# Router of a fused attention and expert kernel: each VectorE operation with at most one operand in SBUF, the rest in PSUM; mask, 1e-9 and counts folded into other tiles

## The chip, the cores and the metric

The kernel runs on one core of a Trainium2 chip. The metric is the device time of one execution in microseconds (us). The engines are named as the profile names them: PE (TensorE, with PEld for its weight loads), DVE (VectorE), ACT (ScalarE), POOL (GpSimd) and SP (SyncE, which here only issues DMAs). Each engine works through its own instructions in order. A VectorE operation reads and writes SBUF or PSUM; PSUM has eight banks of 2 KB per partition, and TensorE writes its results there.

## The reference

Attention with pooled queries, followed by a layer of eight experts, of which each token uses one:

```
q_pool = q.reshape(8, 8, 576, 2, 64).mean(axis=3)           # 8 batches, 8 heads, 576 queries, 1152 keys
attn   = softmax(q_pool @ k.T / 8)                          # sum + 1e-9 in the denominator
x      = (attn @ v) as [4608, 512]                          # 4608 tokens
logits = x @ w_gate                                         # [4608, 8]
e_idx  = argmax(logits)
probs  = exp(logits - max);  probs /= probs.sum(-1) + 1e-9
eom    = 1 / (1 + exp(-(x @ w_output_gate)))
out[t] = probs[t, e] * eom[t, e] * (relu(x[t] @ w1[e]) @ w2[e]),   e = e_idx[t]
```

All of it is float32. The kernel splits each matmul operand into a high and a low part.

## The kernel before

The program has an attention stage and an expert stage behind it.

**Attention.** The work is 32 pairs (a batch and two heads, four pairs to a batch). A pair has 18 score steps (two heads times nine chunks of 128 keys). In a score step PE computes scores for 128 keys and 576 queries into a tile `sps` (L277, L279; two such tiles exist), ACT takes the exponential twice (to `ph`, 16 bits, and to full precision, L291 and L292 or L283 and L284), and the difference `pl` is made by POOL (L293) or, in six steps of a pair, by DVE (L287). Four steps later PE multiplies `ph` and `pl` with the values (L306 to L308) in bursts of three chunks. Ahead of the scores, by some 15 steps, a generator `mgen` computes row maxima of the next pair: PE writes a tile `mp` of 128 queries by 384 keys (L230), and DVE reduces it (L231). After five or four query tiles the maxima are transposed by PE (L257), split by DVE into two rows `mr` (L260, L261) and sent by SP into two rows of the operand `qb` (a DMA `qb<-mr`), which the first score step of the next pair needs (L279).

**PSUM.** All the small products share a pool `ps_m` of three banks with the tag `mp`: `mp` itself, the transposed maxima, the transposes and logits of the router, the rank counts. A tile is held from its first write to its last use in program order; a new tile takes a bank that is free by then, and PE waits until that bank's last reader has run.

**Router.** When a batch's attention is done, `logits` (L357) and then `router` (L393) run as generators: at each score step the generator goes on to its next `yield`, and after a `yield 1` it goes on only in a step with a burst. Its instructions stand at the end of the step's. The router transposes the logits of 576 tokens into `tl` (L401), finds the best expert of each token by comparisons and reductions of tiles of 128 partitions by 40 (five groups of tokens by eight experts), all of them in SBUF, and makes a one-hot tile in 16 bits, `ohb` (L436). PE counts with it the rank of each token within its expert (L445 to L448, tile `rk`, with the counts so far, `cum`, cast to `cb`, L438). From this come a slot number `posi`, a gate factor in column 512 of the token rows `xb` (L449), the DMA of these rows to DRAM (`xrows`, L453, L454), the new counts `cum` (L459) and five indirect DMAs that scatter token numbers to their slots (L471), one every three steps. Tokens that a group holds twice are taken out by a `mask` (L432) and by a large number `moob` in their slot (L467). Seven of the eight routers run under the next batch's attention. The eighth runs after the last score step, on its own, and with it the first expert tile waits.

**Order.** PE, DVE, ACT and POOL take their instructions in the order in which the main loop and its generators issue them; `prep_at` places the loads and splits of the pair after next by a table. SP's order follows from the order of the issues.

**Experts.** Tiles of 256 tokens are gathered by slot, multiplied by the weights of their expert (L753, L765 to L767) and scattered to the output. An early tile's gather is set up in the sixth batch's router (`setup`, L617), so that PE has work while the last router finishes.

## Time and profile before

| | |
|---|---|
| time, median of 3 runs | 1728.94 us (1724.48 to 1751.34) |
| the profiled execution | 1714.96 us |
| its span, first to last instruction | 1713.2 us |
| PE busy | 1549.7 us (90%) |
| DVE busy | 1125.6 us (66%), 2246 instructions |
| ACT busy | 1083.1 us (63%) |
| POOL busy | 995.4 us (58%) |

A group of instructions is shown with its line, engine, operation, `out<-in`, count, busy time, mean length of one in ns, and then the idle time of the engine ahead of it with what ended that. In a piece of the timeline a row holds start and length in us, and in brackets the idle time before it. SPq is the queue in which SP issues DMAs. The PE clock is given as a share of full speed.

### The profile page before, as it was taken

To read this page: it belongs to the slowest core of one execution; us is meant where nothing else is said; L and a number is where in the kernel's file an instruction comes from. 1 tells how busy PE (TensorE), PEld (TensorE's weight loads), DVE (VectorE), ACT (ScalarE), POOL (GpSimd) and SP (SyncE) were. 2 spreads that over 40 slices of the span, in tenths; PEclk is the share of its full clock that TensorE was granted. 3 is DMA by queue.
4 is the path that set the end of the run, shared out by engine and by line. 5 is a ranking of instruction groups with operands and counts; after the bars stand their busy time and mean duration, and the time that the engine had idled before them with its cause. 6 is when DMAs were issued, how large, how long until landed. Compare 5 with 4: busy or idle time off the path is not lost. (4 is left out here: it accounts for less than half of the span.)

```text
span 1713.2 us, 42162 instructions
## 1 busy us (share of the span) xinstructions
PE 1549.7 (90%) x16618; PEld 1415.5 (83%) x16618; DVE 1125.6 (66%) x2246; ACT 1083.1 (63%) x1862; POOL 995.4 (58%) x918
## 2 busy tenths in 40 slices
PE   3999988988999898999899889887999999999997
PEld 3888878877888887888888888776899999999996
DVE  3666676675677667667667767766466666666663
ACT  2787777776777777777687767773345444445441
POOL 4678768867777777876777786753322232322210
PEclk8999999999999999999999999988899999999998
DMA  8445554555445644556445653452753663553500
GB/s 215 132 110 148 160 135 106 142 155 138 117 110 163 146 134 133 123 152 167 111 111 144 160 149 106 106 149 78 266 185 129 210 219 123 169 185 127 194 33 23
DMA packets 86401, 242.52 MB, mean 142 GB/s; under 512 B 14314, under 2 KB 15018, under 8 KB 86194
## 3 DMA queue, kind: packets, MB, share of 16 engines
q1 hardware_dynamic: 76474, 218.74, 45.3%
q0 software_dynamic: 9728, 21.05, 3.8%
q8 instruction: 134, 2.20, 0.6%
q14 instruction: 65, 0.53, 0.2%
HBM read 164.70 MB, written 21.17 MB: 108 GB/s over the span
## 5 line engine op out<-in xcount | busy, mean ns | idle before, releaser
L293 POOL TENSOR_TENSOR pl<-p,ph 128x576 f16<-128x576 f32 x381 | 489.9, 1293 | 263.1 <-ACT ph L292 197.7
L231 DVE TENSOR_REDUCE pm<-mp 128x1 f32<-128x384 f32 x864 | 454.2, 550 | 176.5 <-PE mp L230 172.3
L277 PE MATMUL sps<-qa,ka 128*128 128x288 f32 x1152 | 278.7, 324 | 99.4 <-DVE pl L287 47.9
L291 ACT ACTIVATE p<-sps 128x576 f32<-128x576 f32 x381 | 248.4, 652 | 161.3 <-PE sps L279 151.0
L230 PE MATMUL mp<-ka,qa 128*128 128x384 f32 x960 | 317.1, 346 | 10.4 <-DMA qa<-yq 7.9
L277 PEld LDWEIGHTS sps<-qa,ka 128*128 128x128 f32 x1152 | 189.0, 192 | 145.0 <-ACT ph L292 65.5
L306 PE MATMUL av<-vt,ph 128*128 128x65 f16 x2880 | 291.6, 195 | 0.0
L308 PE MATMUL av<-vt,pl 128*128 128x65 f16 x2880 | 289.7, 194 | 0.6 <-POOL pl L293 0.5
L307 PE MATMUL av<-vt,ph 128*128 128x64 f16 x2880 | 290.1, 196 | 0.0
L306 PEld LDWEIGHTS <-ph 128*128 128x128 f16 x2880 | 268.7, 99 | 25.5 <-issue 24.8
L308 PEld LDWEIGHTS <-pl 128*128 128x128 f16 x2880 | 268.4, 100 | 0.9 <-POOL pl L293 0.8
L307 PEld LDWEIGHTS <-ph 128*128 128x128 f16 x2880 | 268.3, 98 | 0.0
L279 PE MATMUL sps<-qb,kb 68*128 68x288 f32 x1152 | 250.9, 300 | 15.8 <-DMA qb<-mr 15.7
L230 PE MATMUL mp<-kb,qb 66*128 66x384 f32 x768 | 264.3, 344 | 0.6 <-DMA kb<-kp 0.6
L292 ACT ACTIVATE ph<-sps 128x576 f16<-128x576 f32 x381 | 246.5, 647 | 0.0
L279 PEld LDWEIGHTS sps<-qb,kb 68*128 68x128 f32 x1152 | 188.8, 193 | 18.0 <-DMA qb<-mr 17.6
L753 PE MATMUL hps<-xh,w1h 128*128 128x256 f32 x704 | 200.1, 284 | 0.0
L283 ACT ACTIVATE ph<-sps 128x576 f16<-128x576 f32 x195 | 127.6, 654 | 114.5 <-PE sps L279 111.5
L753 PE MATMUL hps<-xl,w1h 128*128 128x256 f32 x704 | 199.9, 284 | 0.0
L753 PE MATMUL hps<-xh,w1l 128*128 128x256 f32 x704 | 199.3, 283 | 0.0
L230 PEld LDWEIGHTS mp<-ka,qa 128*128 128x128 f32 x960 | 181.4, 193 | 14.8 <-issue 8.0
L756 ACT ACTIVATE hh<-hps 128x512 fp32r<-128x512 f32 x88 | 52.7, 598 | 220.7 <-PE hps L753 203.0
(174 smaller groups left out, 3219.3 us busy)
## 6 DMA issues: line engine op xcount, KB each, us to landing
ka<-xk SPq DMA_DIRECT2D x128, 288.0 KB
raw1b<-in_w_dram SPq DMA_DIRECT2D x24, 1024.0 KB
raw2b<-in_w_dram SPq DMA_DIRECT2D x24, 1024.0 KB
raw1a<-in_w_dram SPq DMA_DIRECT2D x22, 1024.0 KB
raw2a<-in_w_dram SPq DMA_DIRECT2D x22, 1024.0 KB
qp<-in_qT_dram SPq DMA_DIRECT2D x32, 576.0 KB
kpf<-in_kT_dram SPq DMA_DIRECT2D x32, 576.0 KB
vp<-in_vL_dram SPq DMA_DIRECT2D x32, 576.0 KB
```

The lines of the kernel that those rows point to most:

```text
L230: nc.tensor.matmul(mp, lhsT=l, rhs=r, start=j == 0, stop=j == len(ops) - 1)
L231: nc.vector.tensor_reduce(out=pm[:, i:i + 1], in_=mp, axis=AX.X, op=ALU.max)
L277: nc.tensor.matmul(sps[:, j, 0:288], lhsT=ka[:, h, ks], rhs=qa[:, o + 288 * j:o + 288 * j + 288], start=True, stop=False)
L279: nc.tensor.matmul(sps[:, j, 0:288], lhsT=kb[:, h, ks], rhs=qb[:, h, 288 * j:288 * j + 288], start=False, stop=True)
L283: nc.scalar.activation(out=ph2, in_=x, func=AF.Exp, scale=1.0 / 16)
L291: nc.scalar.activation(out=p32.rearrange("p (j n) -> p j n", j=2), in_=x, func=AF.Exp, scale=1.0 / 16)
L292: nc.scalar.activation(out=ph2, in_=x, func=AF.Exp, scale=1.0 / 16)
L293: nc.gpsimd.tensor_tensor(out=pl, in0=p32, in1=ph, op=ALU.subtract)
L306: nc.tensor.matmul(av_[:, qb, 0:65], lhsT=hi, rhs=vt[:, h, c, 0:65], start=c == 0 and qb == 0, stop=False)
L307: nc.tensor.matmul(av_[:, qb, 0:64], lhsT=hi, rhs=vt[:, h, c, 66:130], start=False, stop=False)
L308: nc.tensor.matmul(av_[:, qb, 0:65], lhsT=lo, rhs=vt[:, h, c, 0:65], start=False, stop=c == NC - 1 and qb == 4)
L753: nc.tensor.matmul(hp[:, f], lhsT=W1[w][:, c, fs], rhs=d[x][:, c], start=i == 0, stop=i == 11)
```

## The change

Only the router and what feeds it change. The logits `lg`, the comparison `eq`, the index `em`, the sums `sx`, `ps`, `cs` and the ranks with offsets `r1` move from SBUF tiles into free columns of the two PSUM tiles `tl` and `rk` (`cut` makes such a view), so that no VectorE operation has two SBUF operands. The one-hot comparison writes 16 bits at once (L432 of the changed kernel); the mask goes, since `moob` is added to `em` before the comparison (L429). The 1e-9 is a ninth column of two lasting tiles `exg`, set once. The counts `cum` are kept in 16 bits, so that PE reads them as they are. There are fewer yields: the rank counts come six steps earlier, the row DMA about five steps earlier, and the five scatters begin nine steps earlier, in the router's own pair.

```diff
-        mask = bp.tile([128, 5, 8], F32, name="mask")
...
-            nc.gpsimd.memset(mask, 1.0)
-            nc.gpsimd.memset(mask[0:64, 4], 0.0)
+            for x in exg:
+                nc.gpsimd.memset(x, 1e-9)
...
+        exg = [bp.tile([128, 5, 9], F32, name=f"exg{i}") for i in range(2)]
...
+            def cut(x, o, *shape):
+                n = math.prod(shape)
+                v = x[:, o:o + n]
+                return v.rearrange("p (t e) -> p t e", e=shape[-1]) if len(shape) == 2 else v
...
-            nc.vector.tensor_copy(out=lg, in_=tv[:, :, 0:16])
-            nc.vector.tensor_tensor(out=lg, in0=lg, in1=tv[:, :, 16:32], op=ALU.add)
+            tv = cut(tl, 0, 5, 32)
+            lg = cut(tl, 160, 5, 16)
+            lh = sm.tile([128, 5, 16], F32, name="lg", bufs=2)
+            V.tensor_copy(out=lh, in_=tv[:, :, 0:16])
+            V.tensor_tensor(out=lg, in0=lh, in1=tv[:, :, 16:32], op=ALU.add)
             yield
             g, og = lg[:, :, 0:8], lg[:, :, 8:16]
+            eq = cut(tl, 248, 5, 8)
...
+            V.tensor_reduce(out=mx, in_=g, axis=AX.X, op=ALU.max)
+            ex = exg[b % 2]
+            V.tensor_tensor(out=ex[:, :, 0:8], in0=g, in1=b8(mx), op=ALU.subtract)
             yield
-            eq = sm.tile([128, 5, 8], F32, name="eq", bufs=2)
-            nc.vector.tensor_tensor(out=eq, in0=g, in1=b8(mx), op=ALU.is_equal)
...
+            V.tensor_tensor(out=eq, in0=g, in1=b8(mx), op=ALU.is_equal)
+            nc.scalar.activation(out=ex[:, :, 0:8], in_=ex[:, :, 0:8], func=AF.Exp)
+            e2 = sm.tile([128, 5, 8], F32, name="eq", bufs=2)
+            V.tensor_tensor(out=e2, in0=eq, in1=em8, op=ALU.mult)
             yield
...
+            em = cut(tl, 288, 5)
+            V.tensor_reduce(out=em, in_=e2, axis=AX.X, op=ALU.min)
+            V.tensor_tensor(out=em, in0=em, in1=moob, op=ALU.add)
             yield
...
-            nc.vector.tensor_tensor(out=oh, in0=em8, in1=b8(em), op=ALU.is_equal)
-            nc.vector.tensor_scalar(out=sx, in0=sx, scalar1=1e-9, scalar2=None, op0=ALU.add)
-            yield
+            ohb = sm.tile([128, 5, 8], BF16, name="ohb", bufs=2)
+            V.tensor_tensor(out=ohb, in0=em8, in1=b8(em), op=ALU.is_equal)
             so = sm.tile([128, 5, 8], F32, name="so", bufs=2)
-            nc.vector.tensor_tensor(out=so, in0=oh, in1=og, op=ALU.mult)
...
-            nc.vector.tensor_tensor(out=oh, in0=oh, in1=mask, op=ALU.mult)
...
-            nc.vector.tensor_copy(out=ohb, in_=oh)
-            cb = sm.tile([128, 8], BF16, name="cb", bufs=2)
-            nc.vector.tensor_copy(out=cb, in_=cum)
...
+            V.tensor_tensor(out=so, in0=og, in1=ohb, op=ALU.mult)
             yield 1
-            rk = ps_m.tile([128, 512], F32, name="tp", tag="mp")
+            rk = psum()
...
+            nc.tensor.matmul(rv, lhsT=ones, rhs=cum.unsqueeze(1).broadcast_to([128, 5, 8]), start=False, stop=True)
+            sl = sm.tile([128, 5], F32, name="sl", bufs=2)
+            V.tensor_reduce(out=sl, in_=so, axis=AX.X, op=ALU.add)
+            nc.scalar.activation(out=sl, in_=sl, func=AF.Exp, scale=-1.0)
+            yield
+            r1 = cut(rk, 40, 5, 8)
+            V.tensor_tensor(out=r1, in0=rv, in1=eoff, op=ALU.add)
+            r2 = sm.tile([128, 5, 8], F32, name="r1", bufs=2)
+            V.tensor_tensor(out=r2, in0=r1, in1=ohb, op=ALU.mult)
+            yield
+            sx = cut(rk, 80, 5)
+            V.tensor_reduce(out=sx, in_=ex, axis=AX.X, op=ALU.add)
+            V.scalar_tensor_tensor(out=sx, in0=sl, scalar=1.0, in1=sx, op0=ALU.add, op1=ALU.mult)
+            V.reciprocal(out=xb[:, :, 512], in_=sx)
...
+            ps = cut(rk, 88, 5)
+            V.tensor_reduce(out=ps, in_=r2, axis=AX.X, op=ALU.add)
...
+            V.tensor_tensor(out=pi, in0=ps, in1=moob, op=ALU.add)
+            yield
...
+            cs = cut(rk, 96, 8)
+            V.tensor_reduce(out=cs, in_=ohb.rearrange("p t e -> p e t"), axis=AX.X, op=ALU.add)
+            V.tensor_tensor(out=cum, in0=cs, in1=cum, op=ALU.add)
...
-        cum = kp.tile([128, 8], F32, name="cum")
+        cum = kp.tile([128, 8], BF16, name="cum")
```

**Where instructions move.** In the lists below L is the line in the kernel's own file, so the two columns of numbers differ by a few. The first place is DVE in the third batch's router, in the score steps in which the one-hot tile is made. `pl` (L287) is the tile that releases a score tile, `pm` (L231) the reduction that releases a bank of `ps_m`. Before:

```order
L231 TENSOR_REDUCE pm<-mp_6730 128x1
L428 TENSOR_TENSOR so<-oh,lg 128x40
L287 TENSOR_TENSOR pl<-sps_6723,ph 128x576
L231 TENSOR_REDUCE pm<-mp_6752 128x1
L231 TENSOR_REDUCE pm<-mp_6757 128x1
L431 TENSOR_REDUCE sl<-so 128x5
L432 TENSOR_TENSOR oh<-oh,mask 128x40
L231 TENSOR_REDUCE pm<-mp_6777 128x1
L436 CAST ohb<-oh 128x40
L438 CAST cb<-cum 128x8
L231 TENSOR_REDUCE pm<-mp_6798 128x1
```

The same engine at the same place of the changed kernel, where a `tp` among the operands of the router is the PSUM tile `tl` or `rk`:

```order
L231 TENSOR_REDUCE pm<-mp_6629 128x1
L432 TENSOR_TENSOR ohb<-em_72,tp 128x40
L434 TENSOR_TENSOR so<-tp,ohb 128x40
L231 TENSOR_REDUCE pm<-mp_6650 128x1
L231 TENSOR_REDUCE pm<-mp_6654 128x1
L444 TENSOR_REDUCE sl<-so 128x5
L375 TENSOR_TENSOR xl<-tp,xh 128x256
L231 TENSOR_REDUCE pm<-mp_6729 128x1
L448 TENSOR_TENSOR tp<-tp,eoff 128x40
L450 TENSOR_TENSOR r_6735<-tp,ohb 128x40
L287 TENSOR_TENSOR pl<-sps_6722,ph 128x576
```

The two casts are gone, the product `so` stands three steps earlier, and between it and the next `pl` stand the rank operations L448 and L450.

The second place is DVE some steps earlier in the same router, behind the end of a value product (L315 to L321 finish it). Before:

```order
L321 TENSOR_TENSOR xb<-av_6310,r 128x5x64
L411 TENSOR_TENSOR eq<-lg,mx 128x40
L413 TENSOR_TENSOR exg<-lg,mx 128x40
L231 TENSOR_REDUCE pm<-mp_6607 128x1
L231 TENSOR_REDUCE pm<-mp_6611 128x1
L260 TENSOR_SCALAR mr<-tp 4x128
```

After:

```order
L321 TENSOR_TENSOR xb<-av_6301,r 128x5x64
L422 TENSOR_TENSOR tp<-tp,mx 128x40
L425 TENSOR_TENSOR eq<-tp,em_72 128x40
L231 TENSOR_REDUCE pm<-mp_6599 128x1
L231 TENSOR_REDUCE pm<-mp_6603 128x1
L260 TENSOR_SCALAR mr<-tp 4x128
```

Two router operations stand ahead of the two reductions in both. But `tl` is in use here now (it is `tp` in L422), and only two banks of `ps_m` are left to the `mp` tiles and the transposed maxima: from `tl`'s transposes to L434, and again from the rank counts to L467, a stretch of some 20 tiles of the pool in each router.

The third place is SP's queue in the pair of the same router. Before:

```order
L99 DMA ka_119<-xk_6599 64x1152
L127 DMA vp<-in_vL_dram 128x1152
L99 DMA ka_119<-xk_6599 64x1152 x3
L99 DMA qa_122<-xq 64x576
L99 DMA qb_125<-xq 64x576
L453 DMA xrows<-xb 128x4x513
L454 DMA xrows<-xb 64x513
```

After:

```order
L99 DMA ka_119<-xk_6591 64x1152
L457 DMA xrows<-xb 128x4x513
L458 DMA xrows<-xb 64x513
L127 DMA vp<-in_vL_dram 128x1152
L99 DMA ka_119<-xk_6591 64x1152 x3
L99 DMA qa_122<-xq 64x576
L99 DMA qb_125<-xq 64x576
```

The row DMA moves ahead of a value load and five operand DMAs. What follows in both is another `qa` and `qb` and then the two DMAs `qb<-mr`.

42 lines of the change are left out of this document (4 added, 38 removed).

## The prediction

> **What bounds the kernel now.** I read busy time by stage first, then the list of waits of PE.
>
> ```profile
> 41.00:1165.00 1124.00, 1012.01 (x13168) 926.08 (x13168) 775.67 (x1809) 832.13 (x1536) 830.17 (x741) 0.98 0.52 134
> 1205.00:1713.00 508.00, 496.01 (x3207) 452.75 (x3205) 308.77 (x332) 228.59 (x288) 127.65 (x118) 0.99 0.45 155
> PE sps L277 <- DVE pl L287: 47.9, 67, 1.6
> PE sps L277 <- ACT ph L292: 46.2, 61, 1.0
> PE sps L279 <- DMA qb<-mr: 15.7, 8, 7.6
> ```
>
> The first two rows are stretches (start and end, length, then busy time of PE, PEld, DVE, ACT and POOL), the others who waited for whom, with total, count and longest. PE sets the time. In the stage of the experts (1205 to 1713) it works 496 of 508 us, and the change touches nothing there. In the attention stage it works 1012 of 1124 us, and most of the 112 us that it lacks are waits for a score tile to come free, from DVE (47.9 us) or ACT (46.2 us). So a router costs time only where its work on DVE delays something that PE waits for. What one costs is read from the length of a pair, from its first exponential to that of the next pair:
>
> ```profile
> 460.56 0.65 ACT L291 ACTIVATE p<-sps 128x576 f32<-128x576 f32 x1
> 494.21 0.65 ACT L291 ACTIVATE p<-sps 128x576 f32<-128x576 f32 x1
> 530.75 0.65 ACT L291 ACTIVATE p<-sps 128x576 f32<-128x576 f32 x1 [0.20 <-PE sps L279]
> ```
>
> The pair from 460.56 has no router and takes 33.65 us (494.21 − 460.56); the next has the third batch's and takes 36.54. A router under attention costs 2.9 us, seven of them 20 us, about 1.2% of the time: that caps what can be won there. The groups and a piece of the timeline show what in the router is slow.
>
> ```profile
> L436 DVE CAST ohb<-oh 128x40 bf16<-128x40 f32 x8 | 10.1, 1266 | 0.0
> L438 DVE CAST cb<-cum 128x8 bf16<-128x8 f32 x8 | 9.0, 1123 | 0.0
> L428 DVE TENSOR_TENSOR so<-oh,lg 128x40 f32<-128x40 f32 x8 | 8.0, 995 | 0.0
> L461 DVE TENSOR_TENSOR r<-r,oh 128x40 f32<-128x40 f32 x8 | 1.5, 184 | 0.0
> L451 DVE TENSOR_TENSOR r<-tp,eoff 128x40 f32<-128x40 f32 x8 | 1.3, 163 | 0.1
> 509.31 1.11 DVE L428 TENSOR_TENSOR so<-oh,lg 128x40 f32<-128x40 f32 x1
> 512.87 1.42 DVE L436 CAST ohb<-oh 128x40 bf16<-128x40 f32 x1
> 514.21 1.26 DVE L438 CAST cb<-cum 128x8 bf16<-128x8 f32 x1
> 509.12 1.24 POOL L192 TENSOR_TENSOR vt<-vp,vt 128x576 f16<-128x576 f32 x1
> 512.82 1.43 POOL L137 TENSOR_TENSOR yq<-qp 128x576 f32<-128x576 f32 x1
> 514.20 1.25 POOL L192 TENSOR_TENSOR vt<-vp,vt 128x576 f16<-128x576 f32 x1
> ```
>
> Forty elements take 184 ns in L461 and about 1000 to 1270 ns in the two casts and `so`. Each of the three slow ones starts just behind the start of a POOL operation and ends with it (509.12 + 1.24 = 510.36 against 509.31 + 1.11 = 510.42; 514.25 against 514.29; 515.45 against 515.47). They don't compute longer, they wait for POOL. L461 has the same two SBUF operands as `so` and met no POOL operation.
>
> **The change part by part.** *The waits for POOL.* The casts are gone, and `so` gets one PSUM operand. How much of the 3.4 us of these three reaches PE is read by setting the router's pair beside the plain one, matmul by matmul:
>
> ```profile
> 511.24 0.50 PE L277 MATMUL sps<-qa,ka 128*128 128x288 f32 x2 [1.21 <-DVE pl L287]
> 515.08 0.51 PE L277 MATMUL sps<-qa,ka 128*128 128x288 f32 x2
> 517.52 0.50 PE L277 MATMUL sps<-qa,ka 128*128 128x288 f32 x2 [0.74 <-DVE xl L376]
> 476.27 0.50 PE L277 MATMUL sps<-qa,ka 128*128 128x288 f32 x2 [0.58 <-DVE pl L287]
> 480.11 0.51 PE L277 MATMUL sps<-qa,ka 128*128 128x288 f32 x2
> 481.25 0.43 PE L277 MATMUL sps<-qa,ka 128*128 128x288 f32 x2
> ```
>
> Behind `so`, the `pl` that frees a score tile comes late: PE waits 1.21 us instead of 0.58, 0.63 lost. Behind the casts PE needs 2.44 us from one score step to the next (515.08 to 517.52) instead of 1.14: 1.30 lost. Together 1.93 us of the router's 2.9; the rest is mostly PE's own work for it and stays. Seven routers: −13.5 us. This supposes that the new forms do not wait. L451, with one operand in each memory, averaged 163 ns over eight routers, so none of its eight met such a wait; what the SBUF-only reductions and the 16-bit one-hot do beside POOL I take to be the same. The page "SBUF — State Buffer" of the Trainium skill, section "Who interferes with whom", says that an operation with at most one SBUF input, outside the two-port copy modes, does not contend with GpSimd; by that all 20 operations of the new router are free, and the slow rows above agree with its other half.
>
> *The price of a PSUM operand.* 163 ns (L451) against 184 (L461): nothing, at −21 ns for each. The rule that speaks against this change stands in "VectorE: DVE Perf Modes" of the Trainium skill, section "The TRN2 errata": 120 cycles fixed for a PSUM source against 58 from SBUF. At its 0.96 GHz that is an estimated 65 ns for each operation, 0.9 us of DVE per router for some 14 operations, and 6 us in all if PE waited for all of it. The rows say the opposite sign, and I take zero.
>
> *The banks.* This is new work for PE's waits. With `tl` in use, the transposed maxima (L257) must take the bank of the first of the two `mp` tiles just ahead of it, not the third one:
>
> ```profile
> 502.63 0.27 PE L257 MATMUL tp<-ident,m 128*4 128x128 f32 x1
> 504.77 0.53 PE L277 MATMUL sps<-qa,ka 128*128 128x288 f32 x2 [0.76 <-ACT ph L292]
> 502.42 0.34 DVE L411 TENSOR_TENSOR eq<-lg,mx 128x40 f32<-128x40 f32 x1
> 502.79 1.01 DVE L231 TENSOR_REDUCE pm<-mp 128x1 f32<-128x384 f32 x2
> 503.52 0.65 ACT L291 ACTIVATE p<-sps 128x576 f32<-128x576 f32 x1
> ```
>
> The reduction of that tile is the first of the two at 502.79 and ends at about 503.3 (half of 1.01). So L257 goes at 503.35 instead of 502.63, 0.72 us late. Queued behind it on PE is the next score step; ACT starts on that at 503.52 with no idle time before it, and PE waits for ACT's result at 504.77. Nothing on that way has slack, so the 0.72 us is paid in full. In the second hold, that of `rk`, I find one more place: a sum, a product and a reciprocal now stand ahead of a reduction, some 0.6 us by the steps of the last router below; the tile that needs the bank comes later, and I count an estimated 0.15 us of it. Together 0.87 us per router, +6.1 us for seven. The bounds: nothing, if the banks fall otherwise; 3.9 us per router, if six more of the some 20 tiles in the two holds lose 0.5 us each (the rival below).
>
> *The row DMA and the scatters.* Each pair's first score step needs `qb<-mr`:
>
> ```profile
> 387.39 0.50 PE L279 MATMUL sps<-qb,kb 68*128 68x288 f32 x2 [1.57 <-DMA qb<-mr]
> 247.18 0.50 PE L279 MATMUL sps<-qb,kb 68*128 68x288 f32 x2 [0.66 <-DMA qb<-mr]
> 521.93 0.39 SPq L453 DMA_DIRECT2D xrows<-xb  x1
> 525.77 1.59 SPq L99 DMA_DIRECT2D qb<-mr  x2
> ```
>
> The list of waits has 15.7 us of this, of which 7.6 is the start of the program; 8.1 us are left in seven waits. Two of them, 1.57 and 0.66, stand at the end of a router's pair, where the row DMA (over 1 MB: 512 rows of 513 floats) is issued 3.8 us ahead of `qb<-mr`. The change issues it ahead of six more DMAs, so it should be through: −2.2 us. Behind it in SP's queue `vp` and `ka` wait for the reciprocal; they have a pair's time. In return the first scatter moves into the same place. Bounds: −8.1, if all seven waits go, and +8, if as many come. I take −2.
>
> *The last router* has nothing beside it:
>
> ```profile
> 1171.36 0.24 DVE L403 COPY lg<-tp 128x80 f32<-128x80 f32 x1 [0.61 <-PE tp L401]
> 1171.64 0.24 DVE L404 TENSOR_TENSOR lg<-lg,tp 128x80 f32<-128x80 f32 x1
> 1172.26 0.20 DVE L413 TENSOR_TENSOR exg<-lg,mx 128x40 f32<-128x40 f32 x1
> 1172.38 0.20 DVE L416 TENSOR_TENSOR eq<-eq,em 128x40 f32<-128x40 f32 x1
> 1175.32 1.28 DVE L741 TENSOR_TENSOR xl<-xps,xh 128x512 fp32r<-128x512 f32 x2
> 1176.73 0.19 PE L784 MATMUL cp<-cb,ones 128*128 128x8 bf16 x1 [2.48 <-DVE cb L782]
> ```
>
> Operations that depend on the one before start some 0.25 us after it (1171.36, 1171.64), others 0.12 (1172.26, 1172.38). Before, L741, on which PE's restart waits, starts 3.96 us after L403. After, the chain has 15 dependent and four free steps ahead of the last one, 15 × 0.25 + 4 × 0.12 = 4.2, and L741 follows 0.12 later: +0.4 us. If a PSUM result is read sooner or later by 0.05 us, this is −0.4 to +1.1.
>
> Three DVE operations per router fewer, and the constants set once at the start, cost or save nothing on PE.
>
> The sum: −13.5 + 6.1 − 2 + 0.4 = −9 us. The profiled execution took 1714.96 us, 1.8 more than its span, and would take 1706. The median of the three runs is 14 us above that execution; the same −9 gives 1720.
>
> **The rivals.** *Two banks are enough* (20%). PE rarely waits for a bank now: the longest kinds of wait quoted above are for score tiles. If the hold costs nothing and all seven late `qb<-mr` go: −13.5 − 8.1 = −21.6, 1707 us. Against it stands the order of L257 and the reduction above.
>
> *The banks take it back* (17%). The place is the two holds of each router, the price a late bank at every tile that is near its release: 3.9 us per router against 1.93 gained, 7 × 1.97 = +14, 1743 us. It decides from the point at which the hold costs 1.93 us per router, less than three places such as the one shown. For it: ACT and DVE follow PE with no slack there, so a late tile is not made good. Against it: DVE itself loses some 3 us of waiting in the same steps, so its reductions come sooner.
>
> *Nothing arrives* (15%): the new forms wait for POOL as the old did, or ACT (46.2 us of waits already) is what PE waits for next. The step behind `so` speaks against it, where the wait in the plain pair is 0.58 and no other engine has been late: 1729 us.
>
> **How the numbers follow.** My forecast has 48%: 1720 us, with 1712 to 1732 as its own range, from the bounds of the DMA term (−8.1 to +8 where −2 was taken) and of the last router. The range of all cases, from below the first rival to the second, is 1700 to 1742. A measurement of this kernel tells about 2% from no change, some 35 us; no case reaches it, and what is left is for what I have not seen: faster 5%, within 2% 90%, slower 5%.
>
> **What would show it.** Right: no DVE operation of a router averages over 0.35 us; a router's pair lasts about 1.1 us less than 36.54 beside a plain pair of 33.65; L257 of such a pair waits some 0.7 us for the reduction ahead of it. Wrong: the pair keeps its length with short operations (the banks took it), or PE's waits for `qb<-mr` change by more than 8 us, or the time moves by more than 20 us without a change in the pairs, which would put it behind the last router.

## The result, and the profile after

The changed kernel is slower. Its median is 1759.3 us over 20 runs (1748.3 to 1767.0), that of the kernel before 1733.2 us over 20 runs on the same chip; the ratio is 1.016, with a 95% interval of 1.013 to 1.018. On a second chip it was 1.020 (1.016 to 1.024). I had forecast 1720 us, 1700 to 1742. The profiled execution took 1759.9 us with a span of 1758.2, 45.0 more than before. That is more than the 26.1 us between the medians (34.6 on the second chip): the profiled execution of the kernel before, 1715.0 us, was faster than all of its 20 runs, that of the changed kernel stands at its median. So what follows from the two traces has the right places, and sums that are too large.

First the groups of the new router's operations on DVE, from the page's list of groups (the three slowest, and the two that answer to the slow rows of before):

```profile
L413 DVE TENSOR_TENSOR tp<-lg,tp 128x80 f32<-128x80 f32 x8 | 2.0, 245 | 0.3
L412 DVE COPY lg<-tp 128x80 f32<-128x80 f32 x8 | 1.9, 242 | 9.6 <-PE tp L408 9.6
L466 DVE TENSOR_REDUCE tp<-ohb 128x8 f32<-128x40 bf16 x8 | 1.8, 225 | 0.0
L434 DVE TENSOR_TENSOR so<-tp,ohb 128x40 f32<-128x40 f32 x8 | 1.6, 200 | 0.3
L432 DVE TENSOR_TENSOR ohb<-em,tp 128x40 bf16<-128x40 f32 x8 | 1.5, 187 | 0.0
```

None averages over 0.25 us; `so` fell from 995 ns to 200, and the casts of 1266 and 1123 ns are gone. What the change was built to do, it does. The list of PE's waits shows where the time went:

```profile
PE sps L277 <- DVE pl L287: 48.0, 67, 2.5
PE sps L277 <- ACT ph L292: 46.7, 60, 1.1
PE sps L279 <- DMA qb<-mr: 44.3, 10, 8.3
PE tp L257 <- DVE pm L231: 4.0, 7, 0.6
```

The waits for score tiles are as before (47.9 and 46.2). The wait for `qb<-mr`, the row maxima that the first score step of a pair needs, went from 15.7 to 44.3 us. Another, `mp` <- `qa<-xq`, 4.2 us once, is new. The fourth row is the bank hold: seven waits of 0.56 us, one per router. The pair with the third batch's router, the plain pair ahead of it and the one behind, by the starts of their first exponentials and by PE's first matmuls of the pair behind:

```profile
475.38 0.65 ACT L291 ACTIVATE p<-sps 128x576 f32<-128x576 f32 x1
509.09 0.65 ACT L291 ACTIVATE p<-sps 128x576 f32<-128x576 f32 x1
553.27 0.65 ACT L291 ACTIVATE p<-sps 128x576 f32<-128x576 f32 x1 [8.05 <-PE sps L279]
589.97 0.65 ACT L291 ACTIVATE p<-sps 128x576 f32<-128x576 f32 x1
544.39 0.50 PE L277 MATMUL sps<-qa,ka 128*128 128x288 f32 x2 [1.36 <-DVE pl L287]
552.36 0.82 PE L279 MATMUL sps<-qb,kb 68*128 68x288 f32 x2 [7.46 <-DMA qb<-mr]
```

The plain pair takes 33.71 us (33.65 before), the router's pair 44.18 (36.54), the one behind it 36.70 (33.86). PE had done the first half of the next pair's scores at 544.9 and stood still for 7.46 us. The matmul that follows takes 0.82 us for two, where it took 0.44: the clock has fallen. The busy time by stretches (start and end, length, busy time of PE, PEld, DVE, ACT and POOL, then PE clock, DMA share and GB/s) shows this too, first the end of the router's pair and the start of the next in the kernel before, then the same in the changed kernel:

```profile
521.90:530.70 8.80, 7.49 (x83) 6.58 (x83) 6.95 (x20) 6.98 (x14) 4.30 (x6) 1.00 0.92 239
530.70:537.00 6.30, 6.30 (x111) 6.14 (x110) 4.15 (x9) 4.76 (x8) 3.77 (x3) 1.00 0.84 273
```

```profile
528.00:540.00 12.00, 11.43 (x172) 10.24 (x171) 9.20 (x25) 8.76 (x17) 11.57 (x12) 1.00 0.95 206
540.00:553.30 13.30, 4.48 (x40) 3.99 (x37) 2.71 (x5) 3.73 (x10) 5.72 (x5) 0.73 1.06 157
553.30:560.00 6.70, 6.70 (x63) 6.70 (x63) 2.46 (x5) 2.38 (x5) 2.28 (x2) 0.51 0.55 170
```

In both kernels the DMA engines are full at the end of a router's pair (0.92 and 0.95). In the kernel before PE doesn't notice: `qb<-mr` comes just in time. In the changed kernel PE waits, and then runs its first 6.7 us at half clock.

The table is worked out from the starts of the pairs' first exponentials in each trace: the sum of the seven pairs with a router, that of the seven pairs behind them, the start of pair 31 (the last), the rest up to the end of the span, and the time at half clock between the starts of pairs 1 and 31. The waits are the row `qb<-mr` of the list, which holds 6 to 8 us of the program's start in every kernel. The other rows are those of the experiments. Each row is one execution, and those of one kernel differ by 19 to 29 us in all (the ranges above), so a few us between two rows show nothing by themselves; the last column goes by all runs.

| kernel | router's pairs | pairs behind | start of pair 31 | rest | at half clock | waits for `qb<-mr` | ratio to before (95%) |
|---|---|---|---|---|---|---|---|
| before | 259.0 | 246.6 | 1131.2 | 582.0 | 23.9 | 15.7 | 1 |
| changed | 292.3 | 268.7 | 1175.6 | 582.5 | 81.9 | 44.3 | 1.016 (1.013 to 1.018) |
| changed, second chip | 288.0 | 267.4 | 1173.8 | 580.0 | 92.2 | 40.0 | 1.020 (1.016 to 1.024) |
| scatters back | 270.7 | 266.6 | 1163.7 | 581.7 | 75.1 | 36.4 | 1.015 (1.009 to 1.022) |
| row DMAs back | 297.0 | 264.7 | 1177.9 | 580.0 | 85.3 | 52.4 | 1.031 (1.025 to 1.037) |
| both back | 270.2 | 263.3 | 1158.9 | 581.5 | 64.9 | 37.1 | 1.014 (1.007 to 1.021) |
| scatters in a quiet place | 272.3 | 269.9 | 1166.6 | 581.8 | 81.9 | 28.7 | 1.021 (1.015 to 1.027) |
| row DMAs in the next pair | 249.4 | 253.6 | 1131.9 | 583.3 | 30.7 | 18.5 | 0.994 (0.992 to 0.996) |
| the same, in the kernel before | 256.0 | 249.2 | 1131.8 | 582.1 | 30.7 | 15.1 | 0.995 (0.992 to 0.997) |
| before, bank held longer | 270.5 | 255.1 | 1151.8 | 588.9 | 47.8 | 23.4 | 1.017 (1.011 to 1.022) |
| that, row DMAs in the next pair | 261.7 | 248.7 | 1141.6 | 590.6 | 37.5 | 17.0 | 1.003 (1.000 to 1.006) |
| both back, short hold | 277.0 | 260.6 | 1160.3 | 584.9 | 61.4 | 35.2 | 1.019 (1.011 to 1.027) |
| both back, `lg` in SBUF | 266.1 | 257.8 | 1153.9 | 587.5 | 61.4 | 33.6 | 1.019 (1.013 to 1.025) |
| changed, row DMAs in the next pair, scatters left | 249.6 | 290.6 | 1159.5 | 579.9 | 61.4 | 40.7 | 1.010 (1.007 to 1.013) |
| changed, no scatters | 274.6 | 254.3 | 1147.1 | 577.2 | 64.9 | 24.7 | not compared |

Of the 45.0 us of the changed kernel, 44.4 lie ahead of pair 31: +33.3 in the router's pairs, +22.1 in the pairs behind them, −9 in the other sixteen, where the kernel before had waits for `qb<-mr` of its own (2.0 us at pair 11, 0.9 at 23, 1.2 at 28), and −2 in what lies ahead of pair 1. The rest is the same to 0.5 us. The loss is a matter of the attention stage, and of the place where a router's pair meets the next.

### The profile page after: what moved, and what is told of

It reads as the page before. It is cut to its first block, busy times and chain, and to the rows that moved or that the text cites. A ratio compares the mean times of both kernels' runs of the same rounds, so it can differ in the third digit from the quotient of the medians.

```text
span 1758.2 us, 42160 instructions
## 1 busy us (share of the span) xinstructions
PE 1560.7 (89%) x16618; PEld 1427.0 (81%) x16618; DVE 1103.5 (63%) x2222; ACT 1081.9 (62%) x1862; POOL 996.3 (57%) x918
## 5 line engine op out<-in xcount | busy, mean ns | idle before, releaser
L231 DVE TENSOR_REDUCE pm<-mp 128x1 f32<-128x384 f32 x864 | 454.8, 551 | 220.4 <-PE mp L230 217.3
L306 PE MATMUL av<-vt,ph 128*128 128x65 f16 x2880 | 296.0, 196 | 0.0
L307 PE MATMUL av<-vt,ph 128*128 128x64 f16 x2880 | 294.5, 197 | 0.0
L308 PE MATMUL av<-vt,pl 128*128 128x65 f16 x2880 | 294.0, 195 | 0.0
L279 PE MATMUL sps<-qb,kb 68*128 68x288 f32 x1152 | 253.9, 303 | 44.3 <-DMA qb<-mr 44.3
L306 PEld LDWEIGHTS <-ph 128*128 128x128 f16 x2880 | 271.8, 100 | 25.9 <-issue 25.4
L307 PEld LDWEIGHTS <-ph 128*128 128x128 f16 x2880 | 271.1, 99 | 0.0
## 6 DMA issues: line engine op xcount, KB each, us to landing
ka<-xk SPq DMA_DIRECT2D x128, 288.0 KB
```

Of the source, the lines that this page charges most:

```text
L231: nc.vector.tensor_reduce(out=pm[:, i:i + 1], in_=mp, axis=AX.X, op=ALU.max)
L279: nc.tensor.matmul(sps[:, j, 0:288], lhsT=kb[:, h, ks], rhs=qb[:, h, 288 * j:288 * j + 288], start=False, stop=True)
L306: nc.tensor.matmul(av_[:, qb, 0:65], lhsT=hi, rhs=vt[:, h, c, 0:65], start=c == 0 and qb == 0, stop=False)
L307: nc.tensor.matmul(av_[:, qb, 0:64], lhsT=hi, rhs=vt[:, h, c, 66:130], start=False, stop=False)
L308: nc.tensor.matmul(av_[:, qb, 0:65], lhsT=lo, rhs=vt[:, h, c, 0:65], start=False, stop=c == NC - 1 and qb == 4)
```

## The experiments

Every ratio is to runs of the kernel before on the same chip. The kernel before issues its two row DMAs (`xrows`, 1026 and 128 KB) 27.7 us into a router's pair, the changed kernel 19.4 us (20.8 in two of the seven). The scatters stand at steps 3, 6, 10, 12 and 15 of the next pair before, and at 12 and 15 of the router's own pair and 1, 3 and 7 of the next in the changed kernel.

### First theory: the scatters, or the row DMA

My first reading was that the two scatters now beside `qb<-mr` delay it. The rival was that the row DMA, now ahead of six more DMAs, holds those up. Four kernels move them one by one. The scatters back:

```diff
+            late = b < nb - 1
+            for _ in range(7 if late else 0):
+                yield
             for t in range(5):
```

> The changed kernel with seven steps of waiting put ahead of the first scatter of seven of the eight routers (the last router is left as it is), so that the scatters stand at the steps where the kernel before has them (3, 6, 10, 12 and 15 of the pair behind the router's); the row DMA keeps the changed kernel's earlier place (issued some 19 us into the router's pair, where it was 28). Scatter theory (the scatters that now fall into steps 12 and 15 of the router's own pair delay the landing of `qb<-mr`): the steady-state waits of PE for `qb<-mr` fall from 37 us to about the 9 us of the kernel before, the seven routers keep their 1.0 us each, and the time is about 7 us below before's (ratio 0.996, 1726 against 1733). Row theory (the row DMA, moved ahead in SyncE's queue, holds up the operands behind it): nothing changes against the changed kernel, waits 30 to 40 us, ratio 1.013 to 1.018. Theory of the tiles in PSUM (bank holds and VectorE forms): the same, ratio 1.015.

Measured: ratio 1.015 (1.009 to 1.022). The row DMAs back (`send` holds the two of them, taken out of their place; `ny` counts from 0):

```diff
             for t in range(5):
                 for _ in range(3):
                     yield
+                    ny += 1
+                    if ny == 2:
+                        send()
```

> The changed kernel with the two row DMAs issued some five steps later, at steps 14 to 16 of the router's pair as in the kernel before; the scatters keep the changed kernel's places (12 and 15 of the router's pair, then 1, 3 and 7 of the next). Scatter theory: waits of PE for `qb<-mr` stay at 30 to 40 us, ratio to before 1.013 to 1.018. Row theory: the waits fall to about 9 us and the ratio to 0.996. If both are needed (the scatters meet what the earlier row DMA has pushed back): waits near 10 us here as well as with the scatters moved back.

Measured: 1.031 (1.025 to 1.037). Both edits together:

> The changed kernel with both moved back, the row DMAs to steps 14 to 16 and the scatters to steps 3, 6, 10, 12 and 15 of the next pair, so that what is left of the change is the VectorE operations, their tiles in PSUM and their earlier steps. Scatter theory and row theory: waits for `qb<-mr` about 9 us, a router's pair 1.0 us shorter than before's, ratio 0.996 (7 us below before). Theory of the tiles in PSUM: ratio 1.015, with the loss in router pairs and not in `qb<-mr`.

Measured: 1.014 (1.007 to 1.021). The scatters at steps 1, 3, 6, 7 and 10 of the next pair, with the seven `yield`s of the first edit and:

```diff
-                for _ in range(3):
+                for _ in range(2 if late else 3):
```

> The changed kernel with the scatters at steps 1, 3, 6, 7 and 10 of the pair behind the router's (seven steps of waiting ahead of the first, two instead of three between them), so that none falls into steps 11 to 17, in which `qb<-mr` of the next pair is sent and the operands of the next pair arrive. Scatter theory: waits for `qb<-mr` below those of the kernel before, 0 to 5 us, ratio 0.990 to 0.995 (1716 to 1724 against 1733). Row theory and theory of the tiles in PSUM: ratio 1.013 to 1.018, waits 30 to 40 us.

Measured: 1.021 (1.015 to 1.027).

Neither theory held as I had put it. The scatters' place makes a difference: 12 us in the start of pair 31 with the row DMAs early (1175.6 to 1163.7), 19 with them late (1177.9 to 1158.9). The place of the row DMAs makes none that shows (1163.7 early, 1158.9 late, scatters back in both). Still the early row DMAs do hold up `qb<-mr`, by a way that I had not thought of. SP uses eight semaphores, counters that a DMA raises when it has landed, in turn for its DMAs, and ahead of each issue it waits until the DMA that used the same semaphore, eight issues ago, has landed. In the third batch's router of the changed kernel (the pair starts at 509.09):

```profile
528.44 0.53 SPq L457 DMA_DIRECT2D xrows<-xb  x1
531.35 0.35 SPq L127 DMA_DIRECT2D vp<-in_vL_dram  x1
538.84 0.56 SPq L99 DMA_DIRECT2D qb<-xq  x1
541.64 1.94 SPq L99 DMA_DIRECT2D qb<-mr  x2
```

Ahead of `qb<-mr` the queue stands still for 2.2 us. The DMA of eight issues ago is `vp`, which stands behind the 1154 KB of the row DMAs; by its semaphore it landed at +32.49 us of the pair, and the first `qb<-mr` went at +32.55. The second waited in the same way for a `ka`: in all seven pairs it went 0.06 to 0.08 us after that had landed, at +32.6 to +35.8, where the kernel before has +32.4 to +32.6. `vp` landed at +30.7 to +33.2, in the kernel before at +25.3 to +26.6. With the row DMAs and the scatters both back the DMA of eight issues ago had landed 1.6 us or more ahead in every router's pair. So the row theory holds for the early place, and moving the row DMAs back swaps this wait for the one of the next section.

With both back PE still waits 1.9 to 3.6 us for `qb<-mr` at the end of each router's pair, where the kernel before waits 0.66 and 1.57 us at two of the seven and not at the others. And the router itself is as short as forecast: score step by score step against the kernel before, steps 0 to 16 of a router's pair are 1.04 us shorter with both back, +0.8 at step 4, +0.2 at step 6, and −0.3, −0.1, −0.1, −0.7 and −0.8 at steps 8 to 12. I had put it at 1.06.

### Second theory: the queue of SyncE has no slack

SP issues its DMAs in order. With the row DMAs late, these are its rows in the router's pair of the third batch, in the kernel before (the pair starts at 494.21), where the rows of `xrows` and `qb<-mr` quoted in the prediction follow, and then with both back (start 502.08). Each time POOL's last `vt` is what `vp` waits for, since `vt` reads the tile that `vp` fills (with both back that `vt` ends at 524.30):

```profile
514.20 1.25 POOL L192 TENSOR_TENSOR vt<-vp,vt 128x576 f16<-128x576 f32 x1
515.47 0.33 SPq L127 DMA_DIRECT2D vp<-in_vL_dram  x1
515.85 2.35 SPq L99 DMA_DIRECT2D ka<-xk  x3
518.29 1.67 SPq L99 DMA_DIRECT2D qa<-xq  x1
520.01 0.91 SPq L99 DMA_DIRECT2D qb<-xq  x1
522.94 1.36 SPq L99 DMA_DIRECT2D qa<-xq  x1
524.40 1.28 SPq L99 DMA_DIRECT2D qb<-xq  x1
```

```profile
524.33 0.33 SPq L127 DMA_DIRECT2D vp<-in_vL_dram  x1
530.06 0.55 SPq L467 DMA_DIRECT2D xrows<-xb  x1
531.27 1.58 SPq L99 DMA_DIRECT2D qa<-xq  x1
532.94 1.51 SPq L99 DMA_DIRECT2D qb<-xq  x1
534.55 1.59 SPq L99 DMA_DIRECT2D qb<-mr  x2
```

From `vp` at +21.26 us to `qb<-mr` at +31.56 the queue of the kernel before pauses once, for 1.0 us ahead of `xrows`, which waits for the gate factor (the reciprocal ends at +27.69, the DMA goes at +27.72, and so in all seven routers); a single issue (second column) takes 0.3 to 1.7 us. With both back the factor is long ready (+18.7) and that pause is gone. `vp` goes at +22.25 and `qb<-mr` at +32.47, 1.0 and 0.9 us later: the pause takes up most of the 1.0 us (`xrows` goes 0.26 us later), and the issues from `xrows` on are slower by 0.65 us together. The 1.0 us of `vp` is the +0.8 and +0.2 of steps 4 and 6, the bank hold: POOL works in its order, and its last `vt` comes later by as much. What the change saves, it saves at steps 8 to 12, most of it behind that `vt`, where it brings PE forward but not `vp`. So PE reaches the next pair 1.0 us sooner and `qb<-mr` comes 0.9 us later, and in the kernel before there was hardly anything to spare: in the five routers without a wait the last data of `qb<-mr` moved at +34.2 to +34.9 us, and PE began to use them at +36.0 to +36.3; from last data to use PE needs 1.2 to 1.4 us where it waits for nothing else (the run without scatters, below).

If so, taking the row DMAs, which nobody needs before the experts' stage, out of that queue should remove the loss. They are issued in the next pair instead, behind `qp` and `kpf`; the scatters stand as in the kernel before:

```diff
+            late = b < nb - 1
+
+            def send():
                 r0 = b * NQ
                 nc.sync.dma_start(out=xrows[r0:r0 + 512].rearrange("(t p) n -> p t n", p=128), in_=xb[:, 0:4])
                 nc.sync.dma_start(out=xrows[r0 + 512:r0 + NQ], in_=xb[64:128, 4])
+            if not late:
+                send()
...
             for t in range(5):
-                for _ in range(3):
+                for _ in range(3 + (7 if late and t == 0 else 0)):
                     yield
+                    ny += 1
+                    if late and ny == 15:
+                        send()
```

> The changed kernel with the row DMAs of seven routers taken out of the router's pair: they are issued in the next pair (steps 3 to 5), behind the loads `qp` and `kpf`, and the scatters stand where the kernel before has them. Queue theory (SyncE issues its DMAs in order, and in a router's pair everything from `vp` at +22.2 us to `qb<-mr` at +32.4 us stands one behind the other, the row DMAs among them, so that `qb<-mr` lands after PE needs it): `qb<-mr` is issued at about +30 us, PE's wait for it in router pairs falls from 2 to 4 us to under 0.5 us, the router's pair takes 35.5 us (36.54 less the 1.06 forecast), the pair behind it 33.7 to 34 at full clock, and the ratio to before is 0.988 to 0.995. Scatter theory (or any in which the router's own operations cost the time): as with both moved back, ratio 1.010 to 1.018.

Measured: 0.994 (0.992 to 0.996). SP's queue at the same place (the pair starts at 494.76) and PE at its end:

```profile
517.00 0.33 SPq L127 DMA_DIRECT2D vp<-in_vL_dram  x1
522.55 0.59 SPq L99 DMA_DIRECT2D qa<-xq  x1
523.24 0.55 SPq L99 DMA_DIRECT2D qb<-xq  x1
523.88 1.58 SPq L99 DMA_DIRECT2D qb<-mr  x2
530.50 0.38 SPq L460 DMA_DIRECT2D xrows<-xb  x1
529.31 0.50 PE L277 MATMUL sps<-qa,ka 128*128 128x288 f32 x2 [0.64 <-DVE pl L287]
529.65 0.42 PE L279 MATMUL sps<-qb,kb 68*128 68x288 f32 x2
```

`qb<-mr` is issued at +29.1 instead of +32.5, PE does not wait, and the pair takes 35.41 us. `vp` still goes late, at +22.24; it no longer matters. The edit takes the row DMAs out of the queue and their 1154 KB out of the engines at once. Nearly all of the gain is time in the queue: against the run with both back the second `qb<-mr` goes 3.4 us earlier (+29.98 for +33.34) and its last data move 3.6 us earlier (+32.23 for +35.87). Of the 3.4 us the row DMAs' own issues are 1.2, and the `qa` and `qb` behind them 2.0 (1.58 and 1.51 us against 0.59 and 0.55). Why an issue behind a large transfer takes longer is not settled. The same edit in the kernel before (`ny == 8`, and no `yield`s added):

> The kernel before with the same row DMAs sent in the next pair, nothing else. Queue theory: its router pairs are bound by VectorE and PE (waits for POOL), with `qb<-mr` just in time, so most stay at 36.5 us; pairs 5 and 9, which wait 0.8 and 1.7 us for `qb<-mr`, shorten, and the ratio is 0.993 to 0.999. The gap between this run and the changed kernel with the same edit is then the gain of the VectorE operations, about 7 us. Against the queue theory: ratio 1.000 and `qb<-mr` issued as late as before (+31.6 us).

Measured: 0.995 (0.992 to 0.997), router's pairs of 36.54 to 36.62 us. The two kernels now differ by what the change itself gains: 256.0 − 249.4 = 6.6 us in seven router's pairs, 0.94 us each. In the whole time that gain doesn't show; the intervals overlap, and pairs 6 and 10 take 4.4 us longer in the changed kernel, which waits there for their own second `qb<-mr`.

Next the hold by itself, as one instruction more in the kernel before, at the step where the changed kernel reads the bank last:

```diff
             nc.vector.tensor_reduce(out=sx, in_=ex, axis=AX.X, op=ALU.add)
+            hd = sm.tile([128, 5], F32, name="hd", bufs=2)
+            nc.vector.tensor_copy(out=hd, in_=tl[:, 0:5])
             yield
```

> The kernel before with one VectorE copy of five columns more per router, which reads the bank of the transposed logits at the step where the changed kernel reads it last, so that this bank is held as long as in the changed kernel and nothing else is changed. Queue theory: steps 4 and 6 of a router's pair grow by about 0.8 and 0.2 us, POOL's last `vt` and with it the load `vp` come about 1 us later (+22.2 instead of +21.3), `qb<-mr` is issued at +32.4, PE waits 0.5 to 2 us for it at the end of the router's pair, and where it idles long enough the next pair runs its first steps at half clock: ratio 1.005 to 1.015. If the hold costs only itself, as my prediction had it (0.9 us a router): ratio 1.003, pair 37.4, no waits for `qb<-mr` and no change in `vp` beyond 0.2 us.

Measured: 1.017 (1.011 to 1.022), nearly the loss of the changed kernel, from one copy of five columns. `vp` and the new wait:

```profile
523.93 0.33 SPq L127 DMA_DIRECT2D vp<-in_vL_dram  x1
PE tp L257 <- DVE pm L231: 4.1, 7, 0.6
PE sps L279 <- DMA qb<-mr: 23.4, 14, 8.2
PE hps L755 <- ACT xh L742: 14.9, 1, 14.9
```

The hold costs PE 0.78 us a router (median over steps 0 to 16), `vp` goes at +22.05, `qb<-mr` at +32.35 and later. By the start of pair 31 that is 20.6 us, not the 5.5 of the hold itself. But the way is not the one that I expected. In six of the seven routers the pause ahead of `xrows` stays, 0.9 to 1.1 us: what sets the queue back is the gate factor, which the hold delays like everything else in the pair (+28.50 for +27.69 in the third batch's router), and not `vp`. PE itself is 0.8 us later as well. The wait arises since the last data of `qb<-mr` are later than that, by 1.2 to 2.4 us in the five routers that had no wait before, only 0.8 to 1.5 of it from the issue; why the rest, is not settled. Another 6.9 us lie in the experts' stage, in a wait of 14.9 us for `xh` that this kernel has and the kernel before hasn't; why, is not settled, and the bank is not in use there. Both edits together, the hold with the row DMAs out of the way:

> The kernel before with the extra copy that holds the bank longer, and with the row DMAs of seven routers sent in the next pair: the hold alone (ratio 1.017 with the row DMAs in their place) in a queue that has slack. Queue theory: steps 4 and 6 grow as before (about 0.8 and 0.2 us) and the router's pair is 37.3 to 37.6 us, but `qb<-mr`, issued at about +30 us, is in time, so that there is no wait and no half clock behind it: 1.0 us times seven above the kernel before with the row DMAs in the next pair (0.995), ratio 0.997 to 1.001. If the hold costs by other means than `qb<-mr`: ratio 1.010 or more.

Measured: 1.003 (1.000 to 1.006). Its router's pairs take 37.36 to 37.41 us, no wait for `qb<-mr` in any of them:

```profile
636.84 0.65 ACT L291 ACTIVATE p<-sps 128x576 f32<-128x576 f32 x1
674.21 0.65 ACT L291 ACTIVATE p<-sps 128x576 f32<-128x576 f32 x1 [0.20 <-PE sps L279]
```

That is 261.7 − 256.0 = 5.7 us for seven routers, 0.8 each: with the row DMAs out of the way the hold costs the router's pair itself and no more. (By pair 31 it is 9.8 us; the other 4.1 lie in other pairs, 3.4 of them in pair 27. The same surplus in the experts' stage, 8.6 us, is in this ratio too.) The changed kernel beside these on one chip:

> The changed kernel as it is, beside the others on one chip. All theories: slower than before; from the runs so far (the changed kernel with its row DMAs late 1.031, with its scatters moved back 1.015) ratio 1.015 to 1.030. Queue theory adds: `vp` at +22.2 us of each router's pair against +21.3, waits of PE for `qb<-mr` of 2.5 us or more at the end of each.

Measured: 1.020 (1.016 to 1.024).

### Without the hold

Is the hold all of it? The first try to shorten it takes four `yield`s out ahead of `so` and gives them back behind it, in the kernel with both back:

```diff
             V.tensor_tensor(out=lg, in0=lh, in1=tv[:, :, 16:32], op=ALU.add)
-            yield
...
             V.tensor_tensor(out=so, in0=og, in1=ohb, op=ALU.mult)
+            for _ in range(4):
+                yield
             yield 1
```

> The run with both moved back (row DMAs and scatters at the steps of the kernel before), and the bank of the transposed logits let go early: the router's first four waiting steps are taken out ahead of `so` and given back behind it, so that `so`, the last reader of that bank, stands at step 2 and not at step 6. Queue theory: steps 4 and 6 are back at 1.4 and 2.1 us, POOL's `vt` and the load `vp` at +21.3 to 21.5 us, `qb<-mr` at +31.6; PE would be through the router's pair after 34.5 to 35 us and waits 1.5 to 2.5 us for `qb<-mr`, which lands at about +36.5 as in the kernel before, so the router's pair is no shorter than before's 36.5, and where the idle stretch brings half clock the next pair loses 2 us or more: ratio 1.003 to 1.010, still not faster, though the work is 1.9 us shorter. If only the hold were behind the loss: ratio 0.990 to 0.996.

Measured: 1.019 (1.011 to 1.027), and it says little: with ten small operations in one step, steps 1 and 2 grew by 0.4 and 0.7 us instead of step 4 by 0.8, and `vp` went at +22.55. The second leaves `lg`, `eq` and `em` in SBUF, so that the bank is free at once:

```diff
-            lg = cut(tl, 160, 5, 16)
+            lg = sm.tile([128, 5, 16], F32, name="lgs", bufs=2)
...
-            eq = cut(tl, 248, 5, 8)
+            eq = sm.tile([128, 5, 8], F32, name="eqs", bufs=2)
...
-            em = cut(tl, 288, 5)
+            em = sm.tile([128, 5], F32, name="ems", bufs=2)
```

> The run with both moved back (row DMAs and scatters at the steps of the kernel before), with `lg`, `eq` and `em` in SBUF instead of in the bank of the transposed logits, which so is free after the sum `lg`, as in the kernel before; three operations of a router then read two operands from SBUF again. Queue theory: step 4 of router pairs is back at 1.4 us, `vp` at +21.3 and `qb<-mr` at +31.6 us; PE is through the router's pair by 35 to 36 us and waits 0.5 to 2 us for `qb<-mr`, so the pair stays near before's 36.5 us, with some half clock behind it; start of pair 31 at 1130 to 1145 us (1158.9 with the hold), ratio 1.000 to 1.008. If the hold is not what makes the loss: as with both moved back, ratio 1.014.

Measured: 1.019 (1.013 to 1.025), start of pair 31 at 1153.9 us. The means are as expected: step 4 is back, `vp` goes at +21.45, `qb<-mr` at +31.2 to +31.6 in most routers, and steps 0 to 16 are 1.82 us shorter than before, which is the whole gain of the VectorE operations (I had forecast 1.93). The end is not: PE waits 2.3 to 4.3 us instead of 0.5 to 2, and the router's pairs are longer than before's, not equal.

```profile
823.82 0.49 PE L277 MATMUL sps<-qa,ka 128*128 128x288 f32 x2 [0.64 <-DVE pl L287]
826.76 0.51 PE L279 MATMUL sps<-qb,kb 68*128 68x288 f32 x2 [2.44 <-DMA qb<-mr]
```

That pair started at 790.03. PE is ready for `qb<-mr` at +34.3 and gets it at +36.7. So without the hold the 1.8 us gained turn into a wait of 2.4, and half clock behind it: the pairs behind lose 11 us in all. A shorter router alone could not have gained here, and by the expectation a ratio as high as with the hold speaks against the hold as what makes the changed kernel slower: with the row DMAs where they are, the loss is there with the hold and without it. PE also gets `qb<-mr` 0.6 to 0.9 us later than in the kernel before, though it was issued no later; the DMA engines are as full as they can be there (0.98 in the same stretch with both back), and I have not settled what else they carry first.

### The scatters by themselves

The row DMAs in the next pair and the scatters left where the changed kernel has them, that is the edit of the best kernel so far without its seven added `yield`s:

```diff
-                for _ in range(3 + (7 if late and t == 0 else 0)):
+                for _ in range(3):
```

> The changed kernel with the row DMAs of seven routers sent in the next pair and the scatters left at the changed kernel's steps (12 and 15 of the router's pair). It differs from the run with the row DMAs in the next pair only in the scatters. If scatters beside the operand DMAs cost by themselves (the difference between the changed kernel and the run with both moved back is 15 to 17 us in the start of pair 31): slower than that run by 7 to 17 us, ratio 0.998 to 1.004. If they cost only because `qb<-mr` is late and so goes out beside them: `qb<-mr` is issued at +29 to 30 us, ahead of the second scatter, and the ratio is that of the run with the row DMAs in the next pair, 0.992 to 0.996.

Measured: 1.010 (1.007 to 1.013), 27.6 us in the start of pair 31 above the run that differs in the scatters alone. `qb<-mr` of the router's pair was in time, as expected, but the second one, in the middle of the next pair, was not; one of the seven (issued at 840.10, with scatters at 829.71, 833.42 and 838.66, and the row DMAs in flight), and the stretch up to its end:

```profile
855.96 0.82 PE L279 MATMUL sps<-qb,kb 68*128 68x288 f32 x2 [8.47 <-DMA qb<-mr]
846.00:855.90 9.90, 0.90 (x5) 0.38 (x3) 1.69 (x3) 2.29 (x5) 6.29 (x6) 0.66 0.66 87
```

The DMA engines are busy for two thirds of it and move 87 GB/s, against 112 at a share of 0.52 in the same place of the run with the scatters further back. Leaving out the scatters of seven routers:

```diff
+                if b < nb - 1:
+                    continue
                 i = nc.gpsimd.indirect_dma_start(
...
-            nc.gpsimd.memset(di, NTOK)
+            nc.gpsimd.memset(di, 0)
```

> The changed kernel without the 35 scatters of the first seven routers (the lists of rows stay at row 0, so that the experts' stage works on rows that are not the right ones); the last router's are kept. Only the attention stage, up to the start of pair 31, is compared: 1131 us in the kernel before, 1174 to 1176 in the changed kernel. If the scatters cost by themselves what the runs suggest (some 15 us in the changed kernel) and the hold the rest: start of pair 31 at 1150 to 1160 us, waits of PE for `qb<-mr` of 1.5 to 3.5 us at the end of each router's pair. If scatters are most of it: 1130 to 1140, waits under 1 us.

Start of pair 31 at 1147.1 us, 28.5 less than the changed kernel's 1175.6 and 15.9 above the kernel before, which has its scatters (in a trace faster than its median). PE waits 1.3 to 3.5 us at the end of each router's pair; `qb<-mr` is issued 0.06 to 0.08 us after `vp` and `ka` have landed here too. So the scatters do cost by themselves, and where large transfers are in flight they cost most. What they delay is less the data than the end of the transfer. In the third batch's router of the changed kernel the last data of `qb<-mr` moved at +37.35 us and PE went on at +43.26, 5.9 us later; in the six others the gap was 1.8 to 7.0 us, with the row DMAs back 2.0 to 5.6. With the scatters alone back it is 1.0 to 1.6 us, without scatters 1.2 to 1.4. The page "DMA: Bandwidth & Descriptors" of the Trainium skill, section "Queues, rings and completion order", has a rule that fits: the write that counts up the semaphore of a transfer lands only after every earlier write of the same DMA engine, whichever queue that came from. The gaps agree with it; that it is the scatters' writes it waits for was not shown.

### A version ahead of both

Two more kernels put the scatters at steps 3, 3, 6, 10 and 10 of the next pair, with the row DMAs ahead of `qp` and `kpf`; the second also has the four `yield`s moved behind `so`.

```diff
-                for _ in range(3 + (7 if late and t == 0 else 0)):
+                for _ in range((10 if t == 0 else 2) if late else 3):
...
-                    if late and ny == 15:
+                    if late and ny == 8:
```

> The changed kernel with the row DMAs of seven routers sent at steps 1 to 3 of the next pair, ahead of the loads `qp` and `kpf`, and the scatters at steps 3, 3, 6, 10 and 10, so that none stands beside `qb<-mr` at steps 15 and 16 or at step 12. Queue theory: router pairs of 35.4 us, no waits at the end of pairs 6, 10, ... or at their step 8, ratio 0.988 to 0.993. If the place of the scatters makes no difference: as with the row DMAs in the next pair, 0.994.

> The same, with the bank of the transposed logits let go at step 2 instead of step 6. It prices the bank hold with nothing queued on it: my prediction had it at 0.72 us a router, so the router's pairs take 34.5 to 34.7 us instead of 35.4, and the time is 4 to 7 us below the run without it; ratio 0.983 to 0.990. If the hold costs nothing where `qb<-mr` is in time: the same ratio as without it.

Measured: 0.995 (0.992 to 0.999) and 0.996 (0.992 to 0.999). Neither beats the plain move of the row DMAs, and moving the `yield`s gains nothing here either (router's pairs of 35.7 us against 35.4). The best kernel of the study is the changed one with its row DMAs in the next pair and its scatters at their old steps, 0.994; the kernel before with the same move, 0.995, is as good within the measurement.

## Why the prediction was wrong, point by point

*The waits for POOL, −13.5 us: right.* With the bank released at once, steps 0 to 16 of a router's pair are 1.82 us shorter, 12.7 us in seven; forecast 1.93. `so` with one operand in PSUM takes 200 ns, the like operation in SBUF that the prediction quotes 184: a price of 16 ns, where I had taken none (in the last router, with nothing beside it, `so` took 0.20 us in both kernels). The rule of the Trainium skill that spoke against the change, 120 cycles against 58 in "VectorE: DVE Perf Modes", section "The TRN2 errata", would have made it an estimated 65; these rows don't bear it out.

*The banks, +6.1: the size right, the reach wrong.* L257 waits seven times for the reduction ahead of it, 4.0 us in all, and the hold alone costs 0.8 us a router against 0.87 forecast. But I followed it on ACT and PE only. It also delays what the pair's later steps release: POOL and with it the load `vp`, the gate factor and with it the row DMAs. One copy that did nothing but hold the bank cost 20.6 us by pair 31 with the row DMAs ahead of `qb<-mr`, and in the router's pairs 0.8 us each without.

*The row DMA and the scatters, −2 with bounds of −8.1 and +8: this step failed.* It measured about +52 in the two traces: the start of pair 31 came 44.4 us later although the two terms above gave 7.3 (seven times 1.04) back; by the medians it is some +33 (26.1 + 7.3). Three sentences of it fell. "The change issues it ahead of six more DMAs, so it should be through": it was, its larger part having landed at +28.3 to +30.2 us, but `vp` and `ka` landed behind it, `vp` some 5 to 7 us later than before. "Behind it in SP's queue `vp` and `ka` wait for the reciprocal; they have a pair's time": they have not, as the issue of `qb<-mr` waits for their landing. "In return the first scatter moves into the same place": I saw it and priced it by the waits of before, 1.2 us on the average of seven; the waits at that place became 2.4 to 8.3 us, as `qb<-mr` was issued later and PE went on only 1.8 to 7.0 us behind its last data. And no term was there for what follows a wait: the pairs behind the router's lost 22.1 us, mostly to half clock (47.6 us of it in these seven pairs, where it was 6.9), 4.2 of it in one wait for a `qa`.

*The last router, +0.4: right.* L741 starts 4.57 us behind the first copy, where it was 3.96: +0.6, within its bounds. The rest of the span went from 582.0 to 582.5 us.

*The rivals.* "The banks take it back" had the sign and, at 1743, the nearest time, but not its mechanism: the hold was 0.8 us, not 3.9. "Two banks are enough" counted on fewer waits for `qb<-mr`; they rose. "Nothing arrives" is refuted by the rows of DVE and by the steps. The rival I lacked is "the time saved becomes a wait for `qb<-mr`". The profile of before had what points to it: 3.8 us between the issue of `xrows` and that of `qb<-mr`, waits of 1.57 and 0.66 us at the end of two router's pairs, and a DMA share of 0.92 there. A reader who asks at the end of the stage what arrives next, with how much to spare, and what its issue waits for, can find it.

*What would show it* was well chosen: short operations and L257's wait (0.56 us for 0.7) came out right, the router's pairs took 38.6 to 44.7 us where 1.1 less than 36.54 was forecast, and of the three signs against, "PE's waits for `qb<-mr` change by more than 8 us" came true, with 28.6.

## What to carry to other kernels

Time saved inside a stage counts only up to the next arrival that the stage's end waits for; look up the slack of that arrival, what its issue waits for, and the share of the DMA engines there, before crediting anything. Where that slack is used up a small delay grows: a hold of 0.8 us cost 3 us a router with the row DMAs ahead of `qb<-mr`. And a large transfer that nobody needs soon belongs behind the small one that PE waits for, for issuing it earlier only moved the wait from the queue to the landing of what stood behind it: that move by itself gained in the kernel before (0.995), and with the scatters at their old steps it made the change harmless (0.994).

## What the runs showed of the hardware

*A short wait costs the clock as well.* In all seventeen traces I counted the half clock within 6 us of the end of PE's waits for `qb<-mr`, the start of the program left out. Of 69 waits of 1.4 to 3.5 us, 68 were followed by it; of 31 between 0.7 and 1.4 us, 17; of 25 shorter ones, 5. It came in whole pieces of 3.4 us, mostly one or two together, and the first two score steps of a pair then took 2.2 and 4 us instead of 1.2 and 2.5. One such stretch, from the run with both back, behind a wait of 2.52 us:

```profile
540.60:547.00 6.40, 6.40 (x64) 6.40 (x64) 2.46 (x5) 2.49 (x5) 1.28 (x1) 0.57 0.67 224
```

The page "TensorE: Matmul & The Clock Gate" of the Trainium skill, Part 1, has the clock halved after an idle window of about 3.4 us. The pieces of 3.4 us agree with such a window; the waits that brought it on were shorter, down to 1.4 us, in a stage where PE has other gaps of 0.6 us beside them.

*SP's issues wait for landings.* Ahead of each DMA SP waited for the landing of the one eight issues ago. In the changed kernel the second `qb<-mr` of all seven router's pairs followed that landing by 0.06 to 0.08 us; in the kernel before, with the row DMAs behind these loads, the landing was 2.1 us or more ahead.

*Scatters of 128 single words slow down what is in flight.* With the row DMAs early in both, the gap from the last data of `qb<-mr` to PE was 1.8 to 7.0 us with scatters beside it, and 1.0 to 1.6 us with the scatters back. The DMA share was 1.06 at 157 GB/s at the end of a router's pair of the changed kernel, and 0.92 at 239 GB/s in the same place of the kernel before, whose scatters stand elsewhere.
